# Keeping a step's activations in PSUM until they are split, with a new planned order, in a windowed-attention and gated-MLP kernel

## The chip, the cores and the metric

The kernel runs on one core of a Trainium2 chip. The metric is the device time of one execution in microseconds (us). The core's engines are named as in the profile: PE (TensorE, matmuls; PEld is its weight load), ACT (ScalarE), DVE (VectorE), POOL (GpSimd) and SP (SyncE, which issues all the loads and stores). PE writes PSUM, which has eight banks here called b0 to b7; POOL does not read PSUM in this kernel.

## What is computed

```python
scores = scale * np.matmul(q, k.transpose(0, 1, 3, 2))        # 4 x 8 heads x 768 x 768, head_dim 64
is_global = pos[None, :] < n_global                           # 8
is_local = (rel >= 0) & (rel < n_local)                       # 96
dist = np.where(is_global & ~is_local, n_local, np.abs(rel))
scores = np.where(is_global | is_local, scores - slopes * dist, -1e9)
a = np.exp(scores - max); a = a / (a.sum() + 1e-9)
x = (a @ v) as 3072 tokens x 512
h = x @ w_in                                                  # 512 x 2048
g = h * np.cos(h)
out = g @ w_out                                               # 2048 x 512
```

The weights come as float64, the rest as float32.

## The kernel before

**Tiles.** The 3072 tokens are eight chunks of 384. A chunk's attention is done in four units of two heads each; its MLP is done in 16 steps, one for each 128 of the 2048 columns f of w_in. A unit: scores of four windows of 96 queries against 200 keys into PSUM, two of DVE's operations on each window (`fold`, `least`), the exponentials on ACT, sums, reciprocals and the scaling of the probabilities (`norm`, L608 and L613, on DVE or POOL), transposes on PE (L675), masked copies `pv` (L683, L688), and the product with v (L710). The result x is split in a high half xh (ACT, line 260 in the helper `copy`) and a remainder xl (DVE, L731), both float32 of less precision (fp32r), so that three fast matmuls replace one exact one. The eight units of chunks 0 and 1 (called the early units here) multiply their scores in full float32; later ones split q and k as well (`plan_split`, tiles qs and ks).

**A step** (`plan_step`): the first product h = x w_in of 12 matmuls (`moe1`, L746, "M1" below) into one of the two banks of the class `ph`; then for all 384 tokens ACT makes the turns of h (L763), DVE the angle (L766), ACT the cosine (L769, with a table load when the table changes), DVE the product g = h cos(h) (L804). gh is the cast of g to fp32r (helper `copy`: L260 on ACT, L262 on DVE, L264 on POOL), gl the remainder g - gh (L813, on DVE or POOL). The second product takes three matmuls for each 128 tokens (`moe2`, L757), and adds up over the steps in three more banks.

**Weights** (`plan_weights`). For each f one load of w_in and one of w_out, 512 KB each, as raw float64 words. Six operations make float32 of them and split it: `wlow` (L384 on ACT, L386 on the others), `wsign` (L391 on DVE, L394 on POOL), `wbias` (L400, L402), `wjoin` (L405, DVE), `whigh` (helper `copy`) and `wrest` (L415, the remainder, on DVE or POOL). The split weights stay in SBUF for all chunks.

**Order.** `Plan` sets the order of all work. Each operation has a price for every engine that can do it, a due time, what it comes after, and the buffers (`Slot`) that it uses; `Plan.run` walks through planned time and gives each engine its most urgent ready operation. It also has a notion of turns between DVE and POOL: operations with `port=True` on DVE and all on POOL exclude each other (`self.port`). At the end the instructions are written out in planned order, engine by engine, so that prices and constants decide the order but no time on the chip. `PHASES` sets the order of the steps: chunk 0 with f 0 to 7, chunk 1 with all 16, chunk 0 with the rest, then the other chunks. In `emit`, where PE's row is planned to be empty, filler matmuls on zeros are put in (L1054), up to the planned time `FILL_TO`.

Of the kernel before, what the change touches and what calls it, by code (L numbers as in the profile page):

```python
# [10 lines left out]
F32 = mybir.dt.float32  # L11
# [7 lines left out]
ALU = mybir.AluOpType  # L19
# [26 lines left out]
MARGIN, EACH = 3.2, 3.2  # L46
EARLY = {0: 3000, 1: 6000}
WEIGHT = {PE: 1, ACT: 0.5, DVE: 1.2, POOL: 0.8}

PHASES = [(0, 0, 8), (1, 0, 16), (0, 8, 16)]  # L50

# [8 lines left out]

FILL_TO, FILL_REST, FILL_EACH, FILL_FIRST, FILL_COLD = 45000, 150, 250, 10, 7000


class Slot:


    def __init__(self, cls, make):
        self.cls, self.make = cls, make
        self.users = 0
        self.at = None  # L70
        self._tile = None
# [19 lines left out]
class Plan:  # L91
# [7 lines left out]
    SWITCH = 200  # L99

    def __init__(self, places, free):
        self.ops = []
        self.places = {c: list(v) for c, v in places.items()}
        self.busy = {}
        self.free = dict(free)
        self.port = 0
        self.mode = None
# [22 lines left out]
    def run(self):  # L130
# [13 lines left out]
        t = 0  # L144
# [5 lines left out]
        while todo:  # L150
# [5 lines left out]
            while again:  # L156
                again = False
                for e, f in self.free.items():
# [5 lines left out]
                    for o in ready[e]:  # L164
                        if o.ready > t or (best is not None and o.key >= best.key):
                            continue
                        if held and holds(o, e):
                            continue
                        if len(o.engines) > 1:
                            wait = lambda x: max(t, self.free[x], self.port if holds(o, x) else 0) - t  # L170
                            cost = lambda x: wait(x) + o.engines[x] * WEIGHT[x]
                            if any(cost(x) < cost(e) for x in o.engines if x != e):
                                continue
# [36 lines left out]
                    if holds(o, e):  # L210
                        self.port = end
                    self.free[e] = end
                    heapq.heappush(heap, end)
# [26 lines left out]
class Net:  # L240
# [123 lines left out]
    def plan_weights(self, f):  # L364
# [6 lines left out]
        for kind, src, out in (("wi", cols, self.wi), ("wo", rows, self.wo)):  # L371
# [47 lines left out]
            o = p.op({SP: 470}, dma, extra=1460)  # L419
            o = p.op({ACT: 580, DVE: 500, POOL: 700}, wlow, [o], port=True)  # L420
            o = p.op({DVE: 650, POOL: 1310}, wsign, [o], port=True)
            o = p.op({ACT: 580, DVE: 345, POOL: 640}, wbias, [o], port=True)
# [51 lines left out]
    def plan_unit(self, L, pr):  # L474
# [102 lines left out]

        self.chain("worst", p.op({DVE: 80}, worst, [o for _, o in ttr], [st], due=self.xdue(n, pr), port=True))
        exps = []
# [17 lines left out]

        o = p.op({DVE: 85}, add, exps, [st], port=True)
        o = p.op({DVE: 120}, rec, [o], [st], port=True)
# [171 lines left out]
    def plan_step(self, s, n, f, a, b):  # L771
# [23 lines left out]
        for c0, c1 in pieces:  # L795
            w = c1 - c0
            cs = slice(c0, c1)
            r, h = lambda cs=cs: rr.tile[:, cs], lambda cs=cs: ph.tile[:, cs]
            act, dve, pool = 50 + w * 427 // 512, 70 + w * 535 // 512, 100 + w * 1125 // 512
            o = p.op({ACT: act}, lambda e, r=r, h=h: self.turns(e, r(), h()), [done], [ph, rr])  # L800
            o = p.op({DVE: dve}, lambda e, r=r, h=h: self.angle(e, r(), h()), [o], [ph, rr])
            o = p.op({ACT: act + 135}, lambda e, r=r: self.cosine(e, r()), [o], [rr], table="sin")
            o = p.op(
                {DVE: dve}, lambda e, r=r, h=h: nc.vector.tensor_tensor(r(), h(), r(), op=ALU.mult), [o], [ph, rr]  # L804
            )
            o = self.chain("gh", p.op(
                {DVE: 70 + w * 265 // 512, ACT: 50 + w * 475 // 512, POOL: 100 + w * 490 // 512},
                lambda e, r=r, cs=cs: self.copy(e, gg.tile[0][:, cs], r()), [o], [rr, gg], port=True,
            ))

            def low(e, r=r, cs=cs):
                g = gg.tile
                self.eng(e).tensor_tensor(g[1][:, cs], r(), g[0].bitcast(F32)[:, cs], op=ALU.subtract)  # L813

            g = p.op({DVE: dve, POOL: pool}, low, [o], [rr, gg], port=True)
            for t in range(c0 // P, c1 // P):

# [305 lines left out]
```

## Time and profile before

| | |
|---|---|
| time, median of 3 runs | 706.49 us (705.99 to 707.34) |
| the profiled execution | 704.92 us, its span 703.2 us |
| busy in the span | PE 681.4 us (97%), DVE 506.0 (72%), ACT 450.2 (64%), POOL 140.1 (20%) |
| mean granted TensorE clock | 0.99 of full speed |

The span runs from the first to the last instruction of the profiled execution. A busy PE is counted with the modelled ends of its matmuls, fillers among them. A matmul's duration (some 340 ns for 384 columns) is longer than the distance to the next one, since they are pipelined.

### The profile page before, as it was taken

What the parts mean: (1) busy time and instruction counts of PE and PEld (TensorE: products, weight loads), DVE (VectorE), ACT (ScalarE), POOL (GpSimd) and SP (SyncE); (2) the same over time, 40 slices, a digit from 0 to 9 for tenths busy, and PEclk for the clock granted to TensorE, in tenths of its full rate; (3) what the DMA queues carried; (4) which work ended last, traced back from release to release, by engine and by line L of the source; (5) the groups of instructions that cost most, each with busy time, mean ns of one, the idle gap of its engine ahead of it and who ended that gap; (6) DMA issues with size and microseconds to landing.
All of it is one profiled execution on the core that took longest, in us unless ns stands there. A gap on an engine that the chain in (4) does not pass through costs nothing. (4 is left out here: it accounts for less than half of the span.)

```text
span 703.2 us, 12932 instructions
## 1 busy us (share of the span) xinstructions
PE 681.4 (97%) x4448; PEld 595.5 (85%) x4448; DVE 506.0 (72%) x1531; ACT 450.2 (64%) x1129; POOL 140.1 (20%) x180
## 2 busy tenths in 40 slices
PE   8988899999999999999999999999999999999995
PEld 5666799888898888989888898888889888998994
DVE  7998988997847778478776877568784877733442
ACT  6899996776736666467666666476673666634342
POOL 4565665433002121010000121011000112000000
PEclk8999999999999999999999999999999999999998
DMA  9998600013223322032320422212122300001001
GB/s 296 322 305 255 194 22 25 24 46 84 86 67 98 78 60 59 1 104 66 69 68 1 113 62 59 59 57 71 43 68 69 113 27 2 1 1 46 0 1 50
DMA packets 32603, 55.74 MB, mean 79 GB/s; under 512 B 3472, under 2 KB 18192, under 8 KB 32528
## 3 DMA queue, kind: packets, MB, share of 16 engines
q1 hardware_dynamic: 32528, 54.82, 27.1%
q8 instruction: 37, 0.61, 0.4%
q14 instruction: 38, 0.31, 0.1%
HBM read 48.52 MB, written 6.29 MB: 78 GB/s over the span
## 5 line engine op out<-in xcount | busy, mean ns | idle before, releaser
L746 PE MATMUL bank<-xh,w 128*128 128x384 f32 x1024 | 296.7, 343 | 0.6 <-DVE rr L804 0.6
L757 PE MATMUL bank<-w,gh 128*128 128x512 f32 x768 | 245.5, 401 | 0.0
L746 PEld LDWEIGHTS bank<-xh,w 128*128 128x128 f32 x1024 | 188.7, 188 | 8.0 <-DVE rr L804 1.5
L746 PE MATMUL bank<-xl,w 128*128 128x384 f32 x512 | 173.3, 339 | 0.2 <-DVE xl L731 0.2
L757 PEld LDWEIGHTS bank<-w,gh 128*128 128x128 f32 x768 | 138.3, 188 | 22.1 <-issue 0.5
L757 PE MATMUL bank<-w,gl 128*128 128x512 f32 x384 | 151.5, 395 | 0.0
L763 ACT ACTIVATE rr<-bank 128x384 int32<-128x384 f32 x129 | 62.0, 482 | 130.8 <-PE bank L746 128.9
L766 DVE SCALAR_TENSOR_TENSOR rr<-rr,bank 128x384 f32<-128x384 int32 x129 | 69.9, 542 | 103.3 <-ACT rr L763 102.9
L769 ACT ACTIVATE rr<-rr,half_pi 128x384 f32<-128x384 f32 x129 | 78.6, 613 | 40.2 <-DVE rr L766 38.6
L746 PEld LDWEIGHTS bank<-xl,w 128*128 128x128 f32 x512 | 96.7, 189 | 4.3 <-DVE xl L731 0.4
L804 DVE TENSOR_TENSOR rr<-bank,rr 128x384 f32<-128x384 f32 x129 | 70.6, 551 | 37.7 <-ACT rr L769 37.4
L585 ACT ACTIVATE tt<-tt,st 96x104 f32<-96x104 f32 (+1 forms) x256 | 94.3, 370 | 3.9 <-DVE st L560 3.3
L757 PEld LDWEIGHTS bank<-w,gl 128*128 128x128 f32 x384 | 72.1, 188 | 17.3
L813 DVE TENSOR_TENSOR gl<-rr,gh 128x384 fp32r<-128x384 f32 (+1 forms) x114 | 67.9, 595 | 10.2 <-ACT gh L260 7.4
L264 POOL TENSOR_SCALAR ks<-raw 128x408 fp32r<-128x408 f32 (+1 forms) x34 | 19.4, 570 | 273.7 <-PE bank L538 204.7
L260 ACT CAST gh<-rr 128x384 fp32r<-128x384 f32 (+1 forms) x97 | 49.2, 508 | 27.4 <-DVE rr L804 18.8
L560 DVE CUSTOM_DVE_ANT_0 tt<-bank,dd 96x104 f32<-96x104 f32 (+1 forms) x256 | 55.8, 257 | 2.9
L710 PEld LDWEIGHTS bank<-pv,v 104*64 104x64 f32 (+1 forms) x960 | 42.6, 140 | 12.2 <-issue 7.7
L710 PE MATMUL bank<-pv,v 104*64 104x96 f32 (+1 forms) x960 | 49.1, 254 | 1.2 <-ACT pv L260 1.2
L538 PEld LDWEIGHTS bank<-ks,qs 128*96 128x96 f32 x384 | 45.8, 162 | 4.7 <-issue 0.3
L585 ACT ACTIVATION_READ_ACCUMULATOR tt<-tt,st 96x1 f32 x256 | 48.1, 188 | 0.0
L538 PE MATMUL bank<-ks,qs 128*96 128x200 f32 (+1 forms) x384 | 47.9, 254 | 0.0
(95 smaller groups left out, 705.3 us busy)
## 6 DMA issues: line engine op xcount, KB each, us to landing
raw<-in_qk_dram SPq DMA_DIRECT2D x48, 224.0 KB
raw<-in_qk_dram SPq DMA_DIRECT2D x48, 198.0 KB
raw<-in_w_in_dram SPq DMA_DIRECT2D x16, 512.0 KB
raw<-in_w_out_dram SPq DMA_DIRECT2D x16, 512.0 KB
out_dram<-oo SPq DMA_DIRECT2D x24, 256.0 KB
v<-in_v_dram SPq DMA_DIRECT2D x16, 240.0 KB
v<-in_v_dram SPq DMA_DIRECT2D x16, 192.0 KB
raw<-in_qk_dram SPq DMA_DIRECT2D x4, 448.0 KB
```

Of the source, the lines that this page charges most:

```text
L260: self.nc.scalar.copy(out, x)
L538: nc.tensor.matmul(out, qs[:, m, q0], ks[:, k : k + w], start=m == 0, stop=m == 1)
L560: nc.vector.tensor_tensor_reduce(tt[t // 2].tile[:, t % 2, j, :w], ps.tile[:R, i * WIN : i * WIN + w], self.dd[:, v, :w], op0=ALU.add, op1 ...
L585: nc.scalar.activation(x, x, AF.Exp, bias=st.tile[:, c : c + 1], scale=-1.0, accum_out=st.tile[:, n2 + c : n2 + c + 1])
L710: nc.tensor.matmul(px.tile[j * D : (j + 1) * D, t * R : (t + 1) * R], vs.tile[:k, t + c, hs][:, j * D : (j + 1) * D], pv[:k, c, o : o + R] ...
L746: self.nc.tensor.matmul(ph[:, :CW], self.wi[f][:, w, kk * P : (kk + 1) * P], xx[:, kk, :], start=kk == 0 and m == 0, stop=kk == self.NK - ...
L757: self.nc.tensor.matmul(po, gg[:, ts], self.wo[f][:, w, :], start=start and m == 0, stop=stop and m == 2)
L763: self.nc.scalar.activation(r.bitcast(I32), ph, AF.Copy, scale=1.0 / TWO_PI, bias=0.25)
L766: self.nc.vector.scalar_tensor_tensor(r, r.bitcast(I32), -TWO_PI, ph, op0=ALU.mult, op1=ALU.add)
L769: self.nc.scalar.activation(r, r, AF.Sin, bias=self.half_pi)
L804: {DVE: dve}, lambda e, r=r, h=h: nc.vector.tensor_tensor(r(), h(), r(), op=ALU.mult), [o], [ph, rr]
L813: self.eng(e).tensor_tensor(g[1][:, cs], r(), g[0].bitcast(F32)[:, cs], op=ALU.subtract)
```

## The change

The core of the diff; the lines that only repeat it are left out.

```diff
-EARLY = {0: 3000, 1: 6000}
-WEIGHT = {PE: 1, ACT: 0.5, DVE: 1.2, POOL: 0.8}
-PHASES = [(0, 0, 8), (1, 0, 16), (0, 8, 16)]
+EARLY = {0: 5000, 1: 6000}
+WEIGHT = {PE: 1, ACT: 0.5, DVE: 1.2, POOL: 0.6}
+PHASES = [(0, 0, 6), (1, 0, 16), (0, 6, 16)]
+HOLD = 8
-FILL_TO, FILL_REST, FILL_EACH, FILL_FIRST, FILL_COLD = 45000, 150, 250, 10, 7000
+FILL_TO, FILL_REST, FILL_EACH, FILL_FIRST, FILL_COLD = 100000, 150, 250, 10, 7000
...
+    HAND = 170
...
-                        if held and holds(o, e):
+                        if held and holds(o, e) or e == POOL and self.hand > t:
                             continue
...
                     if holds(o, e):
                         self.port = end
+                        if e == DVE:
+                            self.hand = end + self.HAND
+                            heapq.heappush(heap, self.hand)
...
+            y, home = (h, ph) if s < HOLD else (r, rr)
+            act, dve, pool = 50 + w * 427 // 512, 70 + w * 535 // 512, 120 + w * 1125 // 512
...
             o = p.op(
-                {DVE: dve}, lambda e, r=r, h=h: nc.vector.tensor_tensor(r(), h(), r(), op=ALU.mult), [o], [ph, rr]
+                {DVE: dve}, lambda e, r=r, h=h, y=y: nc.vector.tensor_tensor(y(), h(), r(), op=ALU.mult), [o], [ph, rr]
             )
+            if s < HOLD:
+                ways, rest = {ACT: act, DVE: dve}, {DVE: dve}
+            else:
+                ways = {DVE: 70 + w * 265 // 512, ACT: 50 + w * 475 // 512, POOL: 100 + w * 490 // 512}
+                rest = {DVE: dve, POOL: pool}
             o = self.chain("gh", p.op(
-                {DVE: 70 + w * 265 // 512, ACT: 50 + w * 475 // 512, POOL: 100 + w * 490 // 512},
-                lambda e, r=r, cs=cs: self.copy(e, gg.tile[0][:, cs], r()), [o], [rr, gg], port=True,
+                ways, lambda e, y=y, cs=cs: self.copy(e, gg.tile[0][:, cs], y()), [o], [home, gg], port=s >= HOLD,
             ))
...
-            g = p.op({DVE: dve, POOL: pool}, low, [o], [rr, gg], port=True)
+            g = p.op(rest, low, [o], [home, gg], port=s >= HOLD)
```

In steps 0 to 7 the product g is written back into the bank of h, and gh and gl are made from there, on ACT or DVE alone; the bank is in use until gl is done. The planner now starts POOL 170 ns of planned time after an operation of DVE that excludes it. Some prices of DVE and POOL are raised by 20 to 110 ns, the weight of POOL's time is lowered, the first phase has six steps for eight, and fillers may stand up to 100 us of planned time. Operations with several possible engines therefore land on others. Lines move down in the changed kernel: L804 becomes L814, L813 L827, L415 L423, L746 L754, and L260 L268.

**POOL, in the weights of the first steps.** Its row before (`raw` are weight words, `w<-wu,w` is a weight's remainder, wrest):

```order
L394 TENSOR_SCALAR raw<-raw 128x512 x2
L415 TENSOR_TENSOR w<-wu,w 128x512
L394 TENSOR_SCALAR raw<-raw 128x512
L386 TENSOR_SCALAR raw<-raw 128x512
L402 TENSOR_SCALAR raw<-raw 128x512
L264 TENSOR_SCALAR w<-wu 128x512
```

And now, at the first weights' remainders:

```order
L621 TENSOR_TENSOR tt<-tt,st 96x416
L423 TENSOR_TENSOR w<-wu,w 128x512 x3
L272 TENSOR_SCALAR w<-wu 128x512
L423 TENSOR_TENSOR w<-wu,w 128x512 x2
L410 TENSOR_SCALAR raw<-raw 128x512
L402 TENSOR_SCALAR raw<-raw 128x512
```

The remainders and a scaling of probabilities (L621) moved to POOL. Up to the eighth early unit's xl, DVE has ten remainders before and none now.

**ACT, up to the eighth early unit's cast xh.** Before, from the last exponentials of that unit on (`raw` weight words, `rr` a step's activations):

```order
L769 ACT_TABLE_LOAD
L769 ACTIVATE rr<-rr,half_pi 128x384
L260 CAST w<-wu 128x512
L763 ACTIVATE rr<-bank 128x384
L260 CAST gh<-rr 128x384
L384 ACTIVATE raw<-raw 128x512 x2
L769 ACTIVATE rr<-rr,half_pi 128x384
L384 ACTIVATE raw<-raw 128x512
L763 ACTIVATE rr<-bank 128x384
L260 CAST w<-wu 128x512
L384 ACTIVATE raw<-raw 128x512
L400 ACTIVATE raw<-raw 128x512
```

Now, the end of the same stretch:

```order
L268 CAST w<-wu 128x512
L408 ACTIVATE raw<-raw 128x512 x2
L268 CAST gh<-bank 128x384
L771 ACTIVATE rr<-bank 128x384
L392 ACTIVATE raw<-raw 128x512 x2
L408 ACTIVATE raw<-raw 128x512
L392 ACTIVATE raw<-raw 128x512
L777 ACTIVATE rr<-rr,half_pi 128x384
L408 ACTIVATE raw<-raw 128x512
L268 CAST xh<-bank 128x384
```

ACT has more scalings of weight words in front of the cast, fewer weight casts, and gh comes from a bank.

**DVE, around the eighth early unit's xl.** Before:

```order
L804 TENSOR_TENSOR rr<-bank,rr 128x384
L415 TENSOR_TENSOR w<-wu,w 128x512
L766 SCALAR_TENSOR_TENSOR rr<-rr,bank 128x384
L813 TENSOR_TENSOR gl<-rr,gh 128x384
L731 TENSOR_TENSOR xl<-bank,xh 128x384
```

Now:

```order
L774 SCALAR_TENSOR_TENSOR rr<-rr,bank 128x384
L413 SCALAR_TENSOR_TENSOR wu<-raw 128x512 x2
L814 TENSOR_TENSOR bank<-bank,rr 128x384
L739 TENSOR_TENSOR xl<-bank,xh 128x384
L827 TENSOR_TENSOR gl<-bank,gh 128x384
```

The remainder is gone from the place, the product goes into a bank, and gl reads it from there.

## Rows read from the trace of the kernel before

**Rows 1.** Stretches: start and end us, length; busy us (instructions) of PE, PEld, DVE, ACT, POOL; clock, DMA share, GB/s.

```profile
60.00:80.00 20.00, 16.39 (x141) 13.16 (x141) 19.30 (x63) 19.88 (x50) 12.47 (x13) 1.00 1.02 306
80.00:100.00 20.00, 20.00 (x128) 17.96 (x128) 18.44 (x32) 18.52 (x37) 12.12 (x10) 1.00 0.08 24
100.00:120.00 20.00, 20.00 (x102) 18.15 (x101) 15.01 (x25) 14.47 (x29) 11.61 (x10) 1.00 0.15 41
```

**Rows 2.** PE in order of time: start us, us, engine, line, names, shapes, count, [idle before].

```profile
71.62 0.92 PE L534 MATMUL bank<-raw 64*96 64x200 f32 x8
...
73.36 1.55 PE L710 MATMUL bank<-pv,v 104*64 104x96 f32 x32
...
78.59 0.51 PE L675 MATMUL bank<-ident,tt 96*104 96x96 f32 x4 [2.07 <-DVE tt L613]
...
81.03 0.34 PE L746 MATMUL bank<-xh,w 128*128 128x384 f32 x1
```

**Rows 3.** PE's waits from 80 to 690 us: total us, times, longest us.

```profile
PE bank L675 <- POOL tt L613: 1.1, 3, 0.6
PE bank L675 <- DVE tt L613: 1.1, 5, 0.3
```

**Rows 4.** The chain that ended last, late in the span: start us, us, what.

```profile
681.25 2.09 PE bank L746 x12
683.34 2.09 PE bank L757 x9
```

**Rows 5.** PE's groups from 0 to 78.59 us: shapes, count, busy us, mean ns, idle before.

```profile
L746 PE MATMUL bank<-xh,w 128*128 128x384 f32 x48 | 14.9, 369 | 0.6 <-DVE rr L804 0.6
L534 PE MATMUL bank<-raw 64*96 64x200 f32 x112 | 13.5, 363 | 0.0
L710 PE MATMUL bank<-pv,v 96*64 96x96 f32 x112 | 10.8, 275 | 1.2 <-ACT pv L260 1.2
...
L757 PE MATMUL bank<-w,gh 128*128 128x512 f32 x24 | 8.1, 417 | 0.0
```

**Rows 6.** Stretches, columns as in rows 1.

```profile
0.00:85.36 85.36, 73.19 (x593) 54.33 (x594) 76.96 (x293) 74.85 (x216) 48.93 (x78) 0.94 0.89 280
0.00:85.95 85.95, 73.78 (x596) 54.92 (x597) 77.55 (x295) 75.44 (x217) 49.40 (x79) 0.94 0.89 279
...
50.00:55.00 5.00, 5.00 (x43) 4.42 (x43) 3.79 (x17) 3.69 (x17) 3.21 (x5) 0.66 0.73 229
```

**Rows 7.** ACT in order of time, columns as in rows 2.

```profile
76.46 1.28 ACT L769 ACT_TABLE_LOAD   x1
...
84.89 0.46 ACT L260 CAST xh<-bank 128x384 fp32r<-128x384 f32 x1
...
86.33 1.24 ACT L384 ACTIVATE raw<-raw 128x512 int32<-128x512 uint32 x2
```

**Rows 8.** DVE in order of time.

```profile
85.39 0.56 DVE L731 TENSOR_TENSOR xl<-bank,xh 128x384 fp32r<-128x384 f32 x1
85.91 0.56 DVE L804 TENSOR_TENSOR rr<-bank,rr 128x384 f32<-128x384 f32 x1
...
89.65 0.55 DVE L813 TENSOR_TENSOR gl<-rr,gh 128x384 fp32r<-128x384 f32 x1
```

**Rows 9.** Lines up to 100 us, min/median/max ns; then two groups of the whole span, mean ns.

```profile
L813 DVE TENSOR_TENSOR gl<-rr,gh x7: 546/777/1225, 41.8 to 96.9; 128x384 fp32r<-128x384 f32 x7
L731 DVE TENSOR_TENSOR xl<-bank,xh x8: 543/546/567, 17.0 to 85.4; 128x384 fp32r<-128x384 f32 x8
L415 DVE TENSOR_TENSOR w<-wu,w x13: 673/681/1252, 28.6 to 98.1; 128x512 fp32r<-128x512 f32 x13
L415 POOL TENSOR_TENSOR w<-wu,w x5: 1275/1292/1307, 34.0 to 90.4; 128x512 fp32r<-128x512 f32 x5
...
L262 DVE CAST gh<-rr 128x384 fp32r<-128x384 f32 x24 | 8.6, 358 | 3.2 <-PE bank L757 2.6
L262 DVE CAST xh<-bank 128x384 fp32r<-128x384 f32 x4 | 2.2, 552 | 2.6 <-PE bank L710 2.6
```

More of the change, by code (lines that the diff above doesn't have):

```diff
@@ L105, in __init__ @@
         self.free = dict(free)
-        self.port = 0
+        self.port = self.hand = 0
         self.mode = None
@@ L166, in run @@
                             continue
-                        if held and holds(o, e):
+                        if held and holds(o, e) or e == POOL and self.hand > t:
                             continue
                         if len(o.engines) > 1:
-                            wait = lambda x: max(t, self.free[x], self.port if holds(o, x) else 0) - t
+                            turn = lambda x: (self.hand if x == POOL else 0, self.port if holds(o, x) else 0)
+                            wait = lambda x: max(t, self.free[x], *turn(x)) - t
                             cost = lambda x: wait(x) + o.engines[x] * WEIGHT[x]
@@ L419, in plan_weights @@
             o = p.op({SP: 470}, dma, extra=1460)
-            o = p.op({ACT: 580, DVE: 500, POOL: 700}, wlow, [o], port=True)
-            o = p.op({DVE: 650, POOL: 1310}, wsign, [o], port=True)
+            o = p.op({ACT: 580, DVE: 500, POOL: 740}, wlow, [o], port=True)
+            o = p.op({DVE: 650, POOL: 1350}, wsign, [o], port=True)
             o = p.op({ACT: 580, DVE: 345, POOL: 640}, wbias, [o], port=True)
@@ L576, in worst @@
             nc.vector.tensor_tensor(self.worst[:R], self.worst[:R], st.tile[:, :n2], op=ALU.max)
-        self.chain("worst", p.op({DVE: 80}, worst, [o for _, o in ttr], [st], due=self.xdue(n, pr), port=True))
+        self.chain("worst", p.op({DVE: 100}, worst, [o for _, o in ttr], [st], due=self.xdue(n, pr), port=True))
         exps = []
@@ L596, in rec @@
             nc.vector.reciprocal(st.tile[:, 2 * n2 :], st.tile[:, n2 : 2 * n2])
-        o = p.op({DVE: 85}, add, exps, [st], port=True)
+        o = p.op({DVE: 195}, add, exps, [st], port=True)
         o = p.op({DVE: 120}, rec, [o], [st], port=True)
@@ L798, in plan_step @@
             r, h = lambda cs=cs: rr.tile[:, cs], lambda cs=cs: ph.tile[:, cs]
-            act, dve, pool = 50 + w * 427 // 512, 70 + w * 535 // 512, 100 + w * 1125 // 512
+            y, home = (h, ph) if s < HOLD else (r, rr)
+            act, dve, pool = 50 + w * 427 // 512, 70 + w * 535 // 512, 120 + w * 1125 // 512
             o = p.op({ACT: act}, lambda e, r=r, h=h: self.turns(e, r(), h()), [done], [ph, rr])
@@ L803, in plan_step, with low @@
             o = p.op(
-                {DVE: dve}, lambda e, r=r, h=h: nc.vector.tensor_tensor(r(), h(), r(), op=ALU.mult), [o], [ph, rr]
+                {DVE: dve}, lambda e, r=r, h=h, y=y: nc.vector.tensor_tensor(y(), h(), r(), op=ALU.mult), [o], [ph, rr]
             )
+            if s < HOLD:
[3 more added lines that the diff above has]
+                rest = {DVE: dve, POOL: pool}
             o = self.chain("gh", p.op(
-                {DVE: 70 + w * 265 // 512, ACT: 50 + w * 475 // 512, POOL: 100 + w * 490 // 512},
-                lambda e, r=r, cs=cs: self.copy(e, gg.tile[0][:, cs], r()), [o], [rr, gg], port=True,
+                ways, lambda e, y=y, cs=cs: self.copy(e, gg.tile[0][:, cs], y()), [o], [home, gg], port=s >= HOLD,
             ))
-            def low(e, r=r, cs=cs):
+            def low(e, y=y, cs=cs):
                 g = gg.tile
-                self.eng(e).tensor_tensor(g[1][:, cs], r(), g[0].bitcast(F32)[:, cs], op=ALU.subtract)
-            g = p.op({DVE: dve, POOL: pool}, low, [o], [rr, gg], port=True)
+                self.eng(e).tensor_tensor(g[1][:, cs], y(), g[0].bitcast(F32)[:, cs], op=ALU.subtract)
+            g = p.op(rest, low, [o], [home, gg], port=s >= HOLD)
             for t in range(c0 // P, c1 // P):
```

## The prediction

> **What bounds the kernel now.** I read the summary first, then the time in stretches, then PE's waits and the order of PE's pieces, and last the busy time of the other engines up to one point. The summary has PE busy 97% of the span, but that holds fillers and matmuls at half the clock, so the stretches tell more. From 80 us on PE is busy in all of its time, with VectorE (DVE) and ScalarE (ACT) below full; from 60 to 80 us it is the other way: DVE and ACT have hardly a gap, and PE stands still for 3.6 of 20 us [rows 1]. PE's last long wait of the start ends at 78.59 us; it is 2.07 us long, for the scaled scores of the eighth unit [rows 2]. From 80 to 690 us it waits 2.2 us for such scalings, in eight pieces, and for hardly anything else [rows 3]. Behind the start the steps run at PE's own pace: 2.09 us for the first product of a step (12 matmuls), 2.09 for the second (9) [rows 4].
>
> So the time is the sum of PE's useful work, of what PE loses in the start, of some 2 us of later waits and of the last stores. The change leaves the useful work alone; what has to be forecast is the loss in the start. Up to 78.59 us PE has done 6 first products (72 matmuls, the 48 with xh are two thirds of them), 4 second ones (36, with 24 on gh), 128 score matmuls, 56 transposes and 208 matmuls with v [rows 5], with the smaller forms added. At the pace of undisturbed pieces (0.92 us for 8 score matmuls, 0.5 for 4 transposes, 1.55 for 32 with v [rows 2]) this is 12.5 + 8.4 + 14.7 + 7.0 + 10.1 = 52.7 us. **PE lost 78.6 - 52.7 = 25.9 us.** The DMA engines were full at that time, yet DVE and ACT were fed [rows 1], so loads are not what it waited for.
>
> **The change, part by part.** It keeps g of steps 0 to 7 in the bank of h, and it orders everything anew.
>
> *The order of steps.* The first phase has 6 steps instead of 8, so chunk 1 begins at step 6, and its first product needs all eight early units. By the new order PE has then done 6 first and 4 second products; in the old one 8 and 5 stand ahead of the first product of chunk 1. 2 x 2.09 + 2.09 = 6.3 us of PE's work no longer fill the start. Useful work ahead of that point in the new order: 12.5 + 8.4 + 14.7 + 16 x 0.5 + 11.6 (240 matmuls with v) = 55.2 us.
>
> *What ACT does up to the eighth unit's xh.* In the trace this cast runs from 84.89 us, and ACT is busy 74.85 us up to its end, so idle 10.5 [rows 6, 7]. Counted in both orders up to that cast, ACT does less: 2 table loads (1.28 each), 4 weight casts (0.6), 4 casts of chunk 2's q and k, 2 of gh, one first turn and one xh (0.46 [rows 7] less the overlap of neighbours, 0.4 each); and more: 4 weight scalings (two take 1.24) and one query scaling. -2.6 - 2.4 - 3.2 + 2.5 + 0.4 = -5.3 us. With the same idle time xh ends at 85.36 - 5.3 = 80.1 us and xl, 0.56 behind it [rows 8], at 80.7. Only the last 3 of the 12 matmuls need this unit, so the product may begin 1.6 us earlier, at 79.1. The loss is 79.1 - 55.2 = 23.9 us: **a gain of 2.0 us**.
>
> *What DVE does up to the eighth xl.* It is busy 77.55 us to 85.95, idle 8.4 [rows 6, 8]. Ten weight remainders go to GpSimd (POOL): 10 x 0.60 (0.68 [rows 9] less overlap), -6.0. Four half-unit scalings go there too: 4 x 0.55 (as other instructions of some 400 columns, L804 [rows 8]), -2.2. Against it the splits of g and one xh add 1.2 (4 gl at 0.54 become 5 gl, one gh and one xh at 0.48), and the rest is -0.7. In all -7.7: xl ends at 78.2, the product starts at 76.6, the loss is 21.4 us and the gain 4.5. ACT is the later of the two, so the moved remainders are worth less than their 6 us.
>
> *The idle time.* Between 50 and 55 us ACT was idle 1.31 us and DVE 1.21, with a granted clock of 0.66 of full speed: part of it at the lower level, 1.2 GHz [rows 6]. The new order puts 55 filler matmuls on PE for 30, some of them in this part. If the clock holds there, ACT arrives 1.3 us earlier and the gain is 3.3 us. Where PE waits anyway a filler costs nothing; without that cover 25 more would take up to 25 x 0.2 us, since a second-product matmul of the same 512 columns takes 2.09/9 = 0.23 [rows 4], some 5 us. I take the middle of clock held and not held: **2.6 us**.
>
> *g in PSUM.* A product that writes PSUM is not in the trace. Its lower end is DVE's product with one PSUM input into SBUF (L804, 0.56 [rows 8]), its upper end twice that, 8 x 0.56 = 4.5 us over eight steps, of which DVE's slack against ACT (4.5 - 2.0 us) hides 2.5. I take the lower end, as xl, with one input in PSUM, is no slower than L804. gl now has one input in PSUM, as xl has: 546 ns, at most 567, while gl from two SBUF tiles took 546 to 1225 with a median of 777 [rows 9]. Eight gl could save up to 8 x 0.23 = 1.8 us of DVE; ACT's bound hides it. In the Trainium skill, the page SBUF — State Buffer (Who interferes with whom) says that a VectorE instruction with two SBUF inputs contends with a GpSimd instruction that reads SBUF, and that one with at most one SBUF input, outside the two-port modes, does not; the trace agrees, by 567 against 1225 ns at the longest.
>
> gh on DVE loses: 358 ns from SBUF, 552 from PSUM at the same width (the cast of xh) [rows 9]. Only 2 of the eight casts go to DVE, 0.4 us under ACT's bound; if all eight did, 1.6 us. The skill's page VectorE: DVE Perf Modes (Why PSUM operands drop a tier) says this against the change: with an operand in PSUM an fp32 copy runs at the single rate. The trace agrees, with a ratio of 1.5.
>
> *POOL.* It takes the remainders at 1292 ns against DVE's 681 [rows 9]. The counted waits decide only the order. POOL was busy 49.4 of 85.95 us [rows 6]; ten remainders more, 12.9 us, make 62, and weight scalings leave it for ACT. It has room if its inputs come in time; if not, PE waits for weights.
>
> *Behind the arrival.* In both orders fifteen steps lie between chunk 1's first step and the last pair of weights. ACT has nine more weight scalings in the whole program (29 for 20), 9 x 0.62 = 5.6 us. It idles 1.5 and 5.5 us in the two stretches from 80 to 120 us [rows 1], which hides that; without this cover PE would lose part of 5.6 us. Later waits and the stores I leave as they are.
>
> **The sum.** The profiled execution took 704.92 us; 704.92 - 2.6 = 702.3. The median of the runs, 706.49, lies 1.57 above it, so I predict 706.49 - 2.6 = **703.9 us**. A difference under 0.2%, 1.4 us, is about what a measurement here can't tell from none.
>
> **The rivals.** *DVE sets the start (0.13).* If ACT's idle time shrinks with DVE's load, the gain is that of DVE, 4.5 us, and 1.2 more if the clock holds: 700.8 to 702.0. For it: some of ACT's idle time is waiting for DVE and POOL. Against it: ACT was idle only 0.1 us between 60 and 80 us [rows 1], so it was full of its own work.
>
> *No change (0.22).* The new order makes ACT wait for weights that POOL now finishes. With 2.6 us more of idle time on ACT, less work and less cover cancel: 706.5, from 705.1 to 707.9.
>
> *Slower by the held bank (0.20).* There are two banks for h. Before, a bank was free after L804; now it holds g until gl is through. In the trace the first product that ends at 81.4 has its L804 done at 86.5 and its gl at 90.2, 8.8 us behind [rows 2, 8]: the hold would be 3.7 us longer. In the new order 0.7 us of second-product matmuls, step 7's first product (2.1) and fifteen second-product matmuls (3.5) lie between the end of step 6's first product and the start of step 8's: 6.3 us. With 8.8 PE waits 2.5 us there and 0.7 at step 9. In steps 2 to 5 the transposes of a unit stand behind a first product on PE, so the longer hold can push the eighth unit by up to 3.7 us as well. 3.2 to 6.9 us, less the gain of 2.6: 707.1 to 710.8, in the middle 709.0. It decides from 4.0 us of such waits on. Against it: in the new order of DVE gh and gl stand close behind L814, and gl was late before because nothing needed it.
>
> *The likeliest (0.45)*: 1.4 to 4 us faster, its own range 702.5 to 705.1.
>
> **How the numbers follow.** Faster by over 0.2%: 0.45 + 0.13 = 0.58; within: 0.22; slower: 0.20. The range goes from DVE's bound with the clock held (700.8, and 0.2 for the runs' spread: 700.6) to near the middle of the held bank's case, 708.6.
>
> **What would show it.** Right: PE's last long wait ends with under 24 us lost; ACT is busy some 70 us up to the eighth xh; gl from PSUM near 550 ns; granted clock 1.0 from 45 to 60 us. Wrong: PE waits for gl (L827) before step 10; ACT has gaps before the eighth xh; the product into PSUM takes well over 0.6 us; PE waits for weights from POOL; or the waits behind 140 us change by more than 1.4.

## The result, and the profile after

The changed kernel takes 695.91 us (median of 4 runs, 695.79 to 696.89) against 706.39 for the kernel before (705.99 to 707.34): a ratio of 0.9855, 95% interval 0.9843 to 0.9867, so 1.45% faster, and below the predicted range. Its profiled execution took 695.79 us, 9.1 us under that of before. By the medians it is 10.5; the profiled execution of the kernel before, 704.92 us, lies 1.5 us under its median, that of the changed kernel 0.1 under its own.

First the summary of the changed kernel (busy us, share of the span, instructions), with the granted clock over the span in 40 slices, 9 being 90% or more.

```profile
PE 680.9 (98%) x4473; PEld 594.3 (86%) x4473; DVE 485.3 (70%) x1477; ACT 459.2 (66%) x1144; POOL 172.0 (25%) x221
PEclk9999999999999999999999999999999999999999
```

POOL has 32 us more to do and DVE 21 less; from 5.2 to 691 us the clock is at its full level throughout. Next, the stretches of the changed kernel that answer to [rows 1, 6], with the same columns.

```profile
60.00:80.00 20.00, 19.85 (x157) 16.46 (x157) 17.79 (x50) 19.93 (x46) 12.42 (x12) 1.00 1.04 285
80.00:100.00 20.00, 20.00 (x102) 18.02 (x101) 16.66 (x28) 20.00 (x41) 11.14 (x11) 1.00 0.04 10
...
0.00:76.33 76.33, 71.52 (x604) 50.30 (x604) 68.31 (x279) 68.92 (x207) 48.88 (x78) 1.00 0.99 299
0.00:76.92 76.92, 72.01 (x605) 50.48 (x605) 68.90 (x280) 69.51 (x208) 49.47 (x79) 1.00 0.99 300
```

Between 60 and 80 us PE stood still for 3.6 us before; now it has a gap of 0.15. The eighth unit's xh ends at 76.33 us for 85.36, its xl at 76.92 for 85.95. Up to xh, ACT is busy 68.92 us, and idle 76.33 - 68.92 = 7.41 for 10.51. Now PE of the changed kernel around the first product of chunk 1, in order of time.

```profile
73.14 1.55 PE L718 MATMUL bank<-pv,v 104*64 104x96 f32 x32
74.62 0.44 PE L754 MATMUL bank<-xh,w 128*128 128x384 f32 x1
...
76.97 0.44 PE L754 MATMUL bank<-xl,w 128*128 128x384 f32 x1 [0.15 <-DVE xl L739]
```

The product begins at 74.62 us; what is left of a wait is 0.15 us for xl. To see where in the program the 9.1 us come, I compare starts of the same step's first product. These are the 13th and the last of the 128 steps, in the kernel before and then in the changed one.

```profile
104.35 0.34 PE L746 MATMUL bank<-xh,w 128*128 128x384 f32 x1
685.26 0.34 PE L746 MATMUL bank<-xh,w 128*128 128x384 f32 x1
```

```profile
98.55 0.34 PE L754 MATMUL bank<-xh,w 128*128 128x384 f32 x1
676.14 0.34 PE L754 MATMUL bank<-xh,w 128*128 128x384 f32 x1
```

I call this difference to the kernel before the lead. It is 5.80 us at the 13th step, where the start is over, and 9.12 at the last: **5.8 us come from the start and 3.3 from the steady part.** The steady part's waits of PE, from 80 to 690 us (us in total, times, longest), answer to [rows 3]:

```profile
PE bank L683 <- POOL tt L616: 1.1, 3, 0.4
```

Half of the named wait is gone, some 1.2 us. The distance of starts shows more of the 3.3 us, because a matmul's modelled end lies behind the start of the next one: behind 90 us, from a second-product matmul to the transpose that follows it, 399 ns in the mean over 18 places before and 239 over 20 now, some 2.9 us in all. Of these, 1.7 us stand in the rows as waits, the others in none. Summed over all 192 transposes between the 13th and the last step, the distance from the matmul ahead of each is 25.1 us before and 22.5 now: 2.6 of the 3.3 us stand there.

### The profile page after: what moved, and what is told of

Read it like the earlier page. It is cut to its first block, busy times and chain, and to the rows that moved or that the text cites. A ratio compares the mean times of both kernels' runs of the same rounds, so it can differ in the third digit from the quotient of the medians.

```text
span 694.1 us, 12978 instructions
## 1 busy us (share of the span) xinstructions
PE 680.9 (98%) x4473; PEld 594.3 (86%) x4473; DVE 485.3 (70%) x1477; ACT 459.2 (66%) x1144; POOL 172.0 (25%) x221
## 4 chain that ended last, share of the span: by engine, by line
PE 84%; ACT 5%; DVE 4%; DMA 4%; POOL 1%; issue 1%; SPq 0%; ACTq 0%; POOLq 0%; DVEq 0%
PE bank L765 36%; PE bank L754 36%; PE bank L546 5%; PE bank L718 5%; PE bank L683 2%; DMA raw<-in_qk_dram 2%; DMA raw<-in_w_out_dram 1%; ACT tt L593 1%; DVE tt L568 1%; POOL tt L616 1%; ACT L593 1%; ACT L777 1%; DVE bank L559 1%; ACT rr L777 0%; ACT raw L408 0%
## 5 line engine op out<-in xcount | busy, mean ns | idle before, releaser
L754 PE MATMUL bank<-xh,w 128*128 128x384 f32 x1024 | 296.9, 342 | 0.0
L754 PEld LDWEIGHTS bank<-xh,w 128*128 128x128 f32 x1024 | 188.2, 188 | 8.3 <-DVE rr L814 0.6
L754 PE MATMUL bank<-xl,w 128*128 128x384 f32 x512 | 172.9, 338 | 0.2 <-DVE xl L739 0.2
L814 DVE TENSOR_TENSOR rr<-bank,rr 128x384 f32<-128x384 f32 (+1 forms) x121 | 66.6, 551 | 48.4 <-ACT rr L777 47.9
L754 PEld LDWEIGHTS bank<-xl,w 128*128 128x128 f32 x512 | 96.4, 188 | 4.3 <-DVE xl L739 0.4
L827 DVE TENSOR_TENSOR gl<-rr,gh 128x384 fp32r<-128x384 f32 x102 | 60.4, 592 | 13.2 <-ACT gh L268 5.7
L268 ACT CAST gh<-rr 128x384 fp32r<-128x384 f32 (+1 forms) x93 | 47.2, 509 | 31.6 <-DVE rr L814 21.8
L718 PEld LDWEIGHTS bank<-pv,v 104*64 104x64 f32 (+1 forms) x960 | 41.1, 136 | 10.9 <-issue 5.6
L718 PE MATMUL bank<-pv,v 104*64 104x96 f32 (+1 forms) x960 | 47.2, 248 | 0.0
```

The costliest lines, as they stand in the source:

```text
L268: self.nc.scalar.copy(out, x)
L718: nc.tensor.matmul(px.tile[j * D : (j + 1) * D, t * R : (t + 1) * R], vs.tile[:k, t + c, hs][:, j * D : (j + 1) * D], pv[:k, c, o : o + R] ...
L754: self.nc.tensor.matmul(ph[:, :CW], self.wi[f][:, w, kk * P : (kk + 1) * P], xx[:, kk, :], start=kk == 0 and m == 0, stop=kk == self.NK - ...
L814: {DVE: dve}, lambda e, r=r, h=h, y=y: nc.vector.tensor_tensor(y(), h(), r(), op=ALU.mult), [o], [ph, rr]
L827: self.eng(e).tensor_tensor(g[1][:, cs], y(), g[0].bitcast(F32)[:, cs], op=ALU.subtract)
```

## The experiments

One table for all. "Lead" is that of the profiled execution; idle is ACT's, up to the end of the eighth unit's xh. Two executions of almost the same order (the change and a5) differ by 0.15 us in the lead. But a lead is that of one execution: the runs of the kernel before spread from 704.0 to 709.3 us in the first of the five sets, so where lead and median differ, both are told. The kernel before had medians of 706.25, 705.45, 705.63, 705.56 and 705.54 us in the five sets of runs. Of the 18 times expected, six came inside a range that was stated (a1, a5, a8, a9, a11 and b2); above all where a constant makes the planner order anew, the size was not foreseen.

| run | median us | ratio to before, 95% interval | lead, 13th / last step | xh ends, ACT idle |
|---|---|---|---|---|
| the change | 695.91 | 0.9855 (0.9843, 0.9867) | 5.80 / 9.12 | 76.33, 7.41 |
| a1_no_later_fillers | 699.98 | 0.9911 (0.988, 0.9943) | 0.22 / 3.45 | 81.92, 12.24 |
| b1_clock_held | 704.93 | 0.9985 (0.9968, 1.0003) | 0.62 / 0.71 | 84.75, 9.76 |
| a11_clock_dip | 699.18 | 0.9894 (0.9864, 0.9923) | 2.43 / 5.68 | 79.70, 10.22 |
| a5_fill45 | 696.07 | 0.9858 (0.9826, 0.9891) | 5.65 / 8.96 | 76.47, 7.66 |
| b4_six_steps | 708.60 | 1.0037 (1.002, 1.0054) | -1.87 / -2.54 | 79.75, 10.00 |
| b5_six_clock | 706.82 | 1.0013 (0.9999, 1.0027) | -2.92 / -2.34 | 80.80, 10.77 |
| a4_eight_steps | 705.36 | 0.9990 (0.9975, 1.0005) | -2.39 / 0.60 | 86.86, 8.66 |
| a8_five_steps | 698.53 | 0.9900 (0.9868, 0.9931) | 4.84 / 6.45 | 73.29, 7.70 |
| a9_early3 | 695.72 | 0.9858 (0.9833, 0.9882) | 7.14 / 9.64 | 70.73, 6.41 |
| a2_g_in_sbuf | 698.66 | 0.9894 (0.9863, 0.9926) | 4.67 / 6.28 | 76.04, 7.44 |
| b2_g_in_psum | 707.29 | 1.0013 (0.9997, 1.003) | -3.61 / -2.48 | 94.18, 13.48 |
| a3_old_count | 700.92 | 0.9930 (0.9902, 0.9958) | 5.85 / 3.99 | 75.63, 7.51 |
| b3_count | 711.10 | 1.0071 (1.0044, 1.0098) | -6.22 / -6.14 | 90.71, 13.84 |
| a6_no_hand | 709.00 | 1.0051 (1.0036, 1.0066) | -0.66 / -3.63 | 78.85, 7.71 |
| a10_old_prices | 706.22 | 1.0004 (0.9991, 1.0018) | -0.38 / -0.97 | 79.73, 8.75 |
| a7_weight08 | 709.88 | 1.0051 (1.0032, 1.0069) | -3.95 / -6.12 | 80.83, 14.83 |
| b6_count_weight | 699.48 | 0.9910 (0.9886, 0.9933) | 2.97 / 5.97 | 88.31, 8.61 |
| a12_halves_dve | 695.39 | 0.9853 (0.9832, 0.9875) | 5.54 / 9.60 | 76.59, 7.59 |

**The clock, in one order of work.** Three runs touch nothing but fillers. The first keeps the changed kernel's first ten only:

```diff
-FILL_TO, FILL_REST, FILL_EACH, FILL_FIRST, FILL_COLD = 100000, 150, 250, 10, 7000
+FILL_TO, FILL_REST, FILL_EACH, FILL_FIRST, FILL_COLD = 9000, 150, 250, 10, 7000
```

> The changed kernel, its order of every engine untouched, with the first ten filler matmuls alone (10 for 55). Theory C (the clock): the start gained most because the granted clock no longer fell; without fillers it falls to the lower level again somewhere between 5 and 60 us, and 3 to 4 us of the 10.5 us come back: 698.5 to 700 us, PE's pace behind the start untouched. Theory O (the order alone: less work for DVE and ACT ahead of the eighth unit, as in my prediction's sum): PE was not the bound in the start, so a slow PE costs nothing there: 695 to 696.5 us.

The second adds 19 to the kernel before:

```diff
+        more = {6: 6, 7: 1, 8: 2, 40: 1, 41: 9}
...
+                n = more.get(nth, n)
...
+                if nth in more:
+                    free = [u.at for u in o.uses if u.at in banks]
...
```

> The kernel before, its order untouched, with 19 more filler matmuls in five places where its trace shows PE waiting ahead of the two stretches at half clock (6, 1 and 2 ahead of the first two transposes and the first product with v at 11 to 13 us; 1 and 9 ahead of the transposes at 46 and 49 us). Theory C: the granted clock stays at 1.0 through 12.9 to 19.7 and 50.4 to 53.8 us, ACT and DVE are fed there, and 2.5 to 4 us are gained: 702.5 to 704 us. Theory O: the clock may hold, the time stays at 706 us within 1.

The third takes 15 out of the changed kernel:

```diff
-                if n > 0 and free:
+                if n > 0 and free and nth not in (7, 8, 33, 34):
...
```

> The changed kernel without 15 of its 55 fillers: those planned at 12 and 14 us and at 41 to 44 us; the order of all other work is untouched. Theory A (the idle time of ScalarE went because the clock was held): the clock falls at some 13 to 20 us and some 47 to 54 us, ScalarE idles 2.5 to 4 us more up to the eighth xh, the time is 698 to 700.5 us. Theory B (the new order hides these two stretches): the clock falls there but ScalarE idles under 1.5 us more; 696 to 697.5 us. If the clock does not fall, neither is told.

In a1 the clock falls for 27 us of the start and 5.6 of its 5.8 us go in the trace; that is its slowest execution (701.50 us), and by the medians 4.1 us go. In b1 the clock holds throughout and 0.6 us come (1.3 by the medians, with an interval that does not exclude none). In a11 it falls at 14.5 to 21.3 and 45.2 to 52.1 us, 13.7 us in all; before it fell at 12.9 to 19.7 and 50.4 to 53.8, 10.2 in all. Of the start's 5.8 us, 3.4 go in a11. Stretches of a11, then of the changed kernel, columns as in [rows 1]:

```profile
0.00:79.70 79.70, 72.55 (x587) 53.13 (x588) 68.66 (x279) 69.48 (x207) 48.71 (x78) 0.91 0.94 292
14.00:21.00 7.00, 6.74 (x53) 4.57 (x48) 5.46 (x28) 5.78 (x23) 3.99 (x6) 0.54 1.06 363
45.00:52.00 7.00, 5.87 (x41) 5.46 (x43) 5.08 (x20) 6.70 (x17) 5.08 (x6) 0.52 0.77 312
```

```profile
13.00:20.00 7.00, 6.34 (x65) 3.96 (x65) 5.89 (x29) 6.44 (x25) 4.39 (x6) 1.00 1.05 374
45.00:52.00 7.00, 7.00 (x70) 5.85 (x69) 6.93 (x24) 6.97 (x18) 5.27 (x6) 1.00 0.85 298
```

With a clock of 0.52 to 0.54, the lower level, DVE and ACT lose too: DVE is busy 5.08 of 7 us where it was busy 6.93.

Why did the same cure do so little in the old order? In b1 the fillers themselves took most of it away. Rows of PE at the same pieces, of the kernel before and of b1:

```profile
20.54 1.39 PE L710 MATMUL bank<-pv,v 96*64 96x96 f32 x28 [0.58 <-ACT pv L260]
48.99 0.51 PE L675 MATMUL bank<-ident,tt 96*104 96x96 f32 x4 [2.13 <-DVE pv L688]
55.25 0.40 PE L757 MATMUL bank<-w,gl 128*128 128x512 f32 x1
```

```profile
19.16 1.39 PE L710 MATMUL bank<-pv,v 96*64 96x96 f32 x28 [1.23 <-ACT pv L260]
47.61 2.12 PE L1058 MATMUL idle<-zeros 128*128 128x512 bf16 x9 [1.84 <-DVE pv L688]
49.79 0.54 PE L675 MATMUL bank<-ident,tt 96*104 96x96 f32 x4
54.43 0.40 PE L757 MATMUL bank<-w,gl 128*128 128x512 f32 x1
```

With the first fall gone b1 is 1.38 us ahead, and it stays so up to 44 us. Then its nine fillers, which use the bank of the transposes behind them, start only when the bank is free, at 47.61 us, and the transposes stand behind 2.12 us of fillers: b1 is 0.80 us behind. DVE now waits 2.08 us for these transposes, and ACT in its turn 1.72 us for DVE:

```profile
50.37 0.56 DVE L683 TENSOR_TENSOR pv<-bank,others 104x384 f32<-104x384 f32 x1 [2.08 <-PE bank L675]
51.86 0.39 ACT L585 ACTIVATE tt<-tt,st 96x104 f32<-96x104 f32 x1 [1.72 <-DVE st L560]
```

With the second fall gone it wins 1.6 us and is 0.8 ahead at 55 us. Three pairs of runs have the same order of pieces on PE and differ in fillers alone. The same reading (the difference of starts of the same piece, in front of a fall and behind it) gives for each fall:

| order of work: clock held, clock falls | the fall, us | its length | what it costs PE |
|---|---|---|---|
| old: b1, before | 12.9 to 19.7 | 6.8 | 1.4 |
| old with six steps: b5, b4 (below) | 13.1 to 19.9 | 6.8 | 1.4 |
| new: the change, a11 | 14.5 to 21.3 | 6.8 | 1.3 |
| old: b1, before | 50.4 to 53.8 | 3.4 | 1.6 |
| old with six steps: b4, b5 | 52.2 to 55.7 | 3.5 | 1.5 |
| old with six steps: b4, b5 | 62.5 to 65.9 | 3.4 | 1.5 |
| new: the change, a11 | 45.2 to 52.1 | 6.9 | 2.6 |

In a11 0.5 of the 1.3 + 2.6 us is given back at 76 to 78 us. **So a fall costs about the same in the old order and in the new one:** some 0.2 us for each us of it early in the start, where PE's row has gaps and fillers, and 0.4 to 0.5 behind 45 us. The two falls of the kernel before cost 1.4 + 1.6 = 3.0 us by this estimate; the 1.6 is read behind b1's own fillers.

**The limit of the fillers.** The first constant back at its old value leaves out three fillers at 53 us.

```diff
-FILL_TO, FILL_REST, FILL_EACH, FILL_FIRST, FILL_COLD = 100000, 150, 250, 10, 7000
+FILL_TO, FILL_REST, FILL_EACH, FILL_FIRST, FILL_COLD = 45000, 150, 250, 10, 7000
```

> The changed kernel with fillers allowed up to 45 us of planned time, as before, which takes out 3 of the 55 filler matmuls, at one place. Theory A (the new order itself has more planned gaps early, and those fillers hold the clock): the granted clock stays at 1.0 in the whole start and the time is within 0.8 us of the changed kernel, 695.5 to 696.9 us. Theory B (the later limit is what holds the clock between 50 and 55 us): the clock falls there for some 3.4 us, as before, and the time is 0.7 to 2 us longer.

Theory A holds: no fall of the clock, no difference. The fillers come from the new order's own planned gaps, not from the later limit.

**Six steps, and EARLY.** Six in the kernel before; the same with 9 fillers more; eight and five in the changed one; EARLY back:

```diff
-PHASES = [(0, 0, 8), (1, 0, 16), (0, 8, 16)]
+PHASES = [(0, 0, 6), (1, 0, 16), (0, 6, 16)]
```

```diff
+        more = {6: 6, 7: 1, 8: 2}
...
```

```diff
-PHASES = [(0, 0, 6), (1, 0, 16), (0, 6, 16)]
+PHASES = [(0, 0, 8), (1, 0, 16), (0, 8, 16)]
```

```diff
-PHASES = [(0, 0, 6), (1, 0, 16), (0, 6, 16)]
+PHASES = [(0, 0, 5), (1, 0, 16), (0, 5, 16)]
```

```diff
-EARLY = {0: 5000, 1: 6000}
+EARLY = {0: 3000, 1: 6000}
```

> The kernel before with six steps in the first phase and nothing else of the change (its own rule places 32 fillers in the new order). The changed kernel with eight steps lost 8.2 us of its start, so the six steps carry it there. Theory A (two steps' activations less ahead of the eighth unit on DVE and ACT decide the start by themselves, with g in SBUF and DVE's remainders): the lead at step 9 is 3 to 6 us and the time 700 to 703.5 us. Theory B (the steps pay only with DVE's relief, the held bank's shorter chain and the clock together): the lead at step 9 is -2 to 1.5 us, the time 704 to 707 us.

> The kernel before with six first steps and 9 fillers more at 11 to 14 us, which hold the clock between 13 and 20 us; its second fall, at 81 to 85 us behind a bank wait of 2.1 us, stays. Theory A (the held clock takes ScalarE's idle time): idle up to the eighth xh 10.0 to 7.5 or less, 2 to 3 us faster than with six steps alone, 705 to 706.5 us. Theory B (in the old choice of engines DVE and ScalarE are full of own work): idle falls by under 1.2 us and the time by under 1; 707 to 709 us.

> The changed kernel with eight steps in the first phase as before. Theory A (the start is set by the arrival of the eighth unit, and with the clock held DVE and ACT bring it as soon as their own work ahead of it allows): two more steps put some 4 us of activations ahead of it on DVE and ACT, but also 6.3 us of PE's work into the start, so the start is 0 to 3 us worse than in the changed kernel: 696 to 699 us. Theory B (the six steps are the gain): the 5.8 us of the start go back to 0 to 1.5, 700 to 702 us.

> The changed kernel with five steps in the first phase. Theory A (the start is the arrival of the eighth unit, and each step less takes some 4 us of ACT's and DVE's work from ahead of it against 2 to 4 us of PE's work that no longer fills the start): as good as six or up to 2 us better, 693.5 to 696.5 us. Theory B (six is where both meet; with five PE runs out of work ahead of the arrival or of weights behind it): 1 to 4 us slower than the changed kernel, 697 to 700 us.

> The changed kernel with EARLY of chunk 0 back at 3000 (the one constant of the change not yet undone). Theory A (each constant only picks one order out of many, and an order is worth what its eighth unit's arrival and its held banks make of it): the start moves by 2 to 8 us to the worse, 698 to 705 us, and the first product of chunk 1 begins when the eighth xl of DVE ends less 1.6 to 2.3 us, or at a wait for gl or for a bank. Theory B (EARLY is of no matter): within 1 us of the changed kernel.

Alone, the six steps lose. ACT's xh comes 5.6 us earlier in b4, but PE then waits for a bank that DVE's product of an earlier step still reads. PE's row of that wait in b4, then a4's for scaled scores, and a7's (its edit stands further down) for the bank that g holds; in brackets the wait:

```profile
81.35 0.69 PE L746 MATMUL bank<-xh,w 128*128 128x384 f32 x1 [2.12 <-DVE rr L804]
```

```profile
79.49 1.49 PE L683 MATMUL bank<-ident,tt 96*104 96x96 f32 x8 [6.18 <-DVE tt L621]
```

```profile
83.67 0.69 PE L754 MATMUL bank<-xh,w 128*128 128x384 f32 x1 [3.88 <-DVE gl L827]
```

With each of these waits the clock is at the lower level for 3.4 to 6.8 us more (0.69 us for a first matmul that takes 0.44 otherwise). b5's fillers held the clock at 13 to 20 us, which put it 1.4 us ahead of b4 up to 52 us, but it fell at 52 and 62 us instead, where b4 has no fall, and lost 3.0 us there (the table above): neither theory is told by its time. With eight steps in the changed kernel ACT is busy 78.2 us ahead of the eighth xh, 9.3 more than with six, and the start's gain is lost. Five bring xh 3 us earlier, with less of PE's work ahead of it, and are 1 us worse in the start. EARLY moves xh by 5.6 us and the time not measurably.

**g in PSUM.** HOLD = 0 in the changed kernel; in the kernel before, HOLD = 8 with the lines of the change that use it.

```diff
-HOLD = 8
+HOLD = 0
```

> The changed kernel with HOLD at 0: g goes to SBUF in all steps, as before; fillers, prices, phases and counted waits as changed (the planner orders anew). If keeping g in PSUM is worth something by itself (DVE's remainder not shut out, up to 1.8 us by my sum, the bank held longer against it): 697 to 698.5 us. If it is worth nothing: 696 us within 1.

> The kernel before with g kept in PSUM in steps 0 to 7 and nothing else of the change (the planner orders anew). Worth something by itself: 704.5 to 706 us. The longer hold of the two banks hurts in the old phases: 707 to 709 us. Worth nothing: 706.4 within 1. Theory C adds: whatever the order, as long as the granted clock still falls in the start, no more than 2 us are gained.

In b2 the held bank is what was feared; PE's waits from 30 to 110 us begin with

```profile
PE bank L748 <- DVE gl L820: 3.9, 2, 2.0
```

In the changed order no such wait is left, and without the hold the planned order is another one, 2.8 us slower at the end. So what keeping g in PSUM is worth by itself, the first thing that the change does, is not shown by these two runs.

**The counting.** The old counting in the changed kernel; the new one in the kernel before; the 170 ns, the prices and the weight each undone alone; counting and weight together in the kernel before. The edits are of this kind:

```diff
-    HAND = 170
+    HAND = 0
...
-WEIGHT = {PE: 1, ACT: 0.5, DVE: 1.2, POOL: 0.6}
+WEIGHT = {PE: 1, ACT: 0.5, DVE: 1.2, POOL: 0.8}
...
-        o = p.op({DVE: 195}, add, exps, [st], port=True)
+        o = p.op({DVE: 85}, add, exps, [st], port=True)
```

> The changed kernel with the planner's old counting: no 170 ns of planned time before GpSimd's turn, and the old prices of DVE and POOL; all else of the change stays (six first steps, EARLY, WEIGHT, fillers, g in PSUM). Theory A: the lead of 3.3 us that the changed kernel wins behind step 19 comes from the counting, since the planner now knows when a scaling on POOL is really done and places the transposes behind it; the lead behind step 19 falls to 0 to 1 us and the time is 698 to 700 us. Theory B: it comes from another choice of engines (the weight of POOL's time) or from the other sequence as such; the lead behind step 19 stays at 2.5 to 4 us and the time at 695 to 697 us.

> The kernel before with the counting alone (170 ns before GpSimd's turn and the raised prices); eight first steps, 45 us of fillers, g in SBUF stay. Theory A: the waits of 2.2 to 2.5 us ahead of transposes go, the lead at the end is 2 to 3.5 us more than at step 19; the start is left within 1.5 us of before: 702 to 704 us. Theory B: nothing behind step 19 changes: 705 to 707 us.

> The changed kernel without the 170 ns ahead of GpSimd's turn, the raised prices kept. Theory A (it is the 170 ns that order the scalings on POOL rightly ahead of the transposes): behind step 19 the lead falls by 1 to 2 us instead of growing by 3.3, as with the whole old counting; 698.5 to 701 us. Theory B (the raised prices do it): the lead behind step 19 still grows by 2.5 to 4 us; 695 to 697 us.

> The changed kernel with the old prices of DVE and POOL, the 170 ns kept. Theory A (the 170 ns order the later transposes; the prices do little there): behind step 19 the lead grows by 2 to 3.5 us as in the changed kernel, whatever the start is; theory B (both are needed): it falls or stays, -2 to 1 us, as without the 170 ns. The start may move by several us either way: 694 to 706 us.

> The changed kernel with the old weight of POOL's time, 0.8. With the counting alone in the kernel before, whose weight is 0.8, POOL took less work and DVE more, and the later waits stayed. Theory A (counting without the lower weight pushes work from POOL back to DVE, and DVE then comes late): DVE is busy 2 to 4 us more up to the eighth xl, the start is 1.5 to 5 us worse and the later gain 0 to 2 us; 698 to 704 us. Theory B (the weight is of no matter): within 1 us of the changed kernel.

> The kernel before with the 170 ns, the raised prices and the lower weight of POOL's time; eight first steps, g in SBUF, its EARLY and fillers up to 45 us stay. Theory A (these three make the later gain, and the rest of the change only the start): behind step 19 the lead grows by 2 to 3.5 us; the start is that of eight steps, -3 to 1 us; 702 to 707 us. Theory B (the later order hangs on the whole change): the lead behind step 19 grows by under 1 us.

Behind the 13th step the change wins 3.3 us. Without the whole counting it loses 1.9, without the 170 ns 3.0, without the prices 0.6, without the weight 2.2. Counting alone in the kernel before wins 0.1, counting and weight together 3.0, and 3.0 more in the start although xh comes 3 us later than before. PE's waits from 80 to 690 us of a6, b3 and b6:

```profile
PE bank L683 <- POOL tt L616: 2.1, 6, 0.4
PE bank L765 <- ACT oo L268: 0.9, 2, 0.6
```

```profile
PE bank L681 <- POOL tt L614: 1.4, 3, 0.5
PE bank L752 <- DVE rr L810: 1.3, 1, 1.3
PE bank L681 <- DVE tt L619: 0.7, 3, 0.3
```

```profile
PE bank L681 <- POOL tt L614: 1.3, 3, 0.4
PE bank L752 <- DVE rr L810: 0.4, 1, 0.4
```

In a6 all 60 scalings behind 95 us stand on POOL, in a3 too, in a10 31; in the changed kernel, b6 and a7 it is 15, in b3 14, in the kernel before 10. The number alone doesn't decide: a7 has that of the changed kernel and not its gain; it loses 2.0 us in two waits for a bank that DVE's product reads and wins nothing behind them. The distances ahead of the 192 transposes add up to 22.8 us in b6, 24.2 in a7, 25.2 in b3, 26.3 in a3, 26.9 in a10 and 29.0 in a6, for 22.5 in the changed kernel and 25.1 before: against the changed kernel, a6 and a10 lose their steady gain there, b3 most of it, a3 and a7 a part.

**The three waits that are left.** The same order, only the six half scalings of chunks 2, 4 and 6 by DVE:

```diff
-                        self.eng(e).tensor_tensor(
+                        self.eng(DVE if n > 1 else e).tensor_tensor(
...
-                elif o.engine == POOL and held_by is not None:
+                elif o.engine == POOL and held_by is not None and new:
```

> The changed kernel in its own order, but the six half scalings of chunks 2, 4 and 6 that stand on POOL (503 to 845 ns each, two in a row) are made by DVE (347 to 368 ns each) in the same place of the plan. Theory A (PE's three waits of 0.21, 0.44 and 0.43 us at 183, 348 and 514 us end with these): they go, PE wins 0.9 to 1.1 us from 514 us on, 694.7 to 695.1 us. Theory B (DVE is late there itself, or the next wait takes their place): 695.7 us or more.

The planner has 850 ns for such a pair on POOL. The groups of the changed kernel from 95 to 700 us (count, busy us, mean ns), POOL and then DVE:

```profile
L616 POOL TENSOR_TENSOR tt<-tt,st 96x208 f32<-96x208 f32 x3 | 2.5, 844 | 0.0
L616 POOL TENSOR_TENSOR tt<-tt,st 96x192 f32<-96x192 f32 x3 | 1.5, 504 | 7.2 <-DVE st L604 7.2
```

```profile
L616 DVE TENSOR_TENSOR tt<-tt,st 96x208 f32<-96x208 f32 x9 | 3.3, 365 | 0.0
L616 DVE TENSOR_TENSOR tt<-tt,st 96x192 f32<-96x192 f32 x9 | 3.1, 348 | 0.0
```

A pair takes 1.35 us there, 0.71 on DVE. In a12 no wait of PE is left between 80 and 690 us, and the lead at the last step is 0.5 us larger than in the changed kernel (0.7 from the 13th on). The waits go as theory A has it, for a little less than the 0.9 us expected; the medians, 695.39 and 695.91, come from different sets of runs and their ratios can't be told apart.

## Why the prediction was wrong

The sign was right and the size was not: 2.6 us forecast, 9.1 found in the traces and 10.5 in the medians. Its four signs of being right all came (19.4 us lost, 68.92 us of ACT, 554 ns for gl, a full clock), so they could not tell 2.6 us from 5.8 in the start. By its steps:

**What bounds the kernel, and the order of steps: right.** By its own formula PE loses 74.62 - 55.2 = 19.4 us of the start, 6.5 less than 25.9; the lead shows 5.8. In the changed kernel the lighter first phase is needed (a4); by itself it is not enough (b4).

**What ACT and DVE do up to the eighth unit: the busy time right, to 1 us.** Forecast 74.85 - 5.3 = 69.55 for ACT, measured 68.92; 77.55 - 7.7 = 69.85 for DVE, measured 68.90.

**The idle time: the step that failed in the start.** It took ACT's 10.5 us as given and credited the clock with half of 1.3 us. ACT idled 7.41. Letting the clock fall again, in the changed order (a11), gives 10.22 us of idle time, xh at 79.70 and 2.43 us won in the start, close to the forecast without the clock, 80.1 and 2.0. So the clock was the term that was mis-sized: 3.4 us by a11, whose falls are longer than before's, and 3.0 by the two falls of before, where 0.65 had been put. Of the 5.8 us some 3 are the clock's, and the other 2.4 to 2.8 the order's, for 2.0 forecast. The step had the price of the fall that it looked at, at 50 to 55 us, about right (1.3 for 1.6) and halved it; and it left out the fall from 12.9 to 19.7 us, worth 1.4, of which the kernel before has this stretch:

```profile
13.00:20.00 7.00, 6.62 (x52) 5.25 (x52) 5.44 (x30) 4.39 (x18) 4.90 (x6) 0.52 1.02 403
```

ACT is idle 2.61 of 7 us there, and 0.56 in the same stretch of the changed kernel.

**The rival that came nearest, by luck.** "DVE sets the start" gave 4.5 us and 1.2 for the clock, 5.7; measured 5.8. But the parts are wrong, 4.5 for 2.4 to 2.8 and 1.2 for some 3, and ACT's idle time did not shrink because DVE's load did: with that load and the clock falling it was 10.22 us (a11) and 12.24 (a1), for 10.51 before.

**g in PSUM: right.** The product into PSUM takes its lower bound and gl from PSUM some 550 ns, as these rows of the changed kernel up to 100 us show (min/median/max ns), which answer to [rows 9]:

```profile
L814 DVE TENSOR_TENSOR bank<-bank,rr x8: 548/556/567, 39.3 to 83.5; 128x384 f32<-128x384 f32 x8
L827 DVE TENSOR_TENSOR gl<-bank,gh x8: 544/554/558, 44.6 to 84.8; 128x384 fp32r<-128x384 f32 x8
```

The sentence from the Trainium skill's page SBUF — State Buffer (Who interferes with whom) agrees again: at most 558 ns with one SBUF input, for up to 1225 with two [rows 9].

**Slower by the held bank: not here, but real.** Its wait came with 3.9 us in b2 and in a7. How close gl follows the product does not decide it by itself: the changed kernel has 1.3 to 5.4 us from the product's end to gl's without such a wait, and at a7's wait it is 1.7. There the product itself comes late.

**POOL has room: right in effect, wrong in size.** Its 62 us became 49.5 up to xl: with the remainders it took, other work left it.

**Behind the arrival.** ACT's added weight scalings were hidden as forecast: ACT is full from 80 to 100 us and PE does not wait. "Later waits and the stores I leave as they are" was the second step that failed, by 3.3 us. The 170 ns, the prices and the weight, which the prediction took for matters of order only, place the scalings so that the transposes wait less: 2.6 of the 3.3 us stand in the distances ahead of them. Each of the three is needed, and together they do it without the rest of the change (3.0 us in b6).

What stays open: what each part of the order, g in PSUM among them, is worth in the start. The runs put it anywhere from -6.2 to 7.1 us, not in sums of parts: the six steps alone lose 1.9 us, counting and weight without them win 3.0, all together 5.8, and the change without its counting 5.85. Each constant picks another order, and its own waits decide. None of these runs is clearly faster than the changed kernel.

## What to carry to other kernels

Price a fall of the clock by the starts of the same pieces in two runs of one order, in front of it and behind it: here it was 0.2 to 0.5 us for each us of the fall, in the old order as in the new one. The idle time of another engine in one stretch gave only a part. Where fillers are put in to hold the clock, look at what stands behind them: nine of them behind a wait took back 2.2 of the 3.0 us that they should have saved. When a planner's prices change, look at the steady part as well: 0.16 us at eighteen places made half as much as the start did, and over a third of it stood in no wait. Don't add up a planner's constants one by one; undo each, and judge the set.

## What the runs showed of the hardware

A fall of PE's clock to the lower level cost PE 1.3 to 1.4 us for 6.8 us early in the start, in three orders of work, and 1.5 to 1.6 for 3.4 behind 50 us (the table above). POOL's scaling of 96x208 took 844 ns at all three places of the changed kernel's steady part, nearly as long as 96x416 (877), while 96x192 took 504. DVE's product takes as long into PSUM as into SBUF: medians of 556 ns (8 of them) and 548 (the 3 that follow up to 100 us).
